# A gated mix of attention and a mixture of experts: experts taken in the order of their loads, and the steps of the score maxima at listed products

## The chip, the cores and the metric

The kernel runs on one core of one Trainium2 chip. The metric is the device time of one execution in microseconds. Before the change it is 1443.31 us, the median of three runs (1442.71 to 1444.89). The engines are called as the profile calls them: PE is TensorE (PEld its weight loads), DVE is VectorE, ACT is ScalarE, POOL is GpSimd, and SP is SyncE, which issues most of the DMAs.

## What is computed

```python
x = A_x                                          # [1, 2048, 448]
g = sigmoid((x * gate_w).sum(-1, keepdims=True))
# a: softmax attention, 16 heads of 28
q, k, v = split(x @ wqkv)                        # per head
a = softmax(q @ k.T * 28 ** -0.5) @ v @ wo
# b: the two best of 8 experts for each token
logits = x @ w_gate
topk = argsort(-logits)[:, :2];  gates = softmax(logits[topk])
for e in range(8):
    w = (gates * (topk == e)).sum(-1)
    b += w * (silu(x @ w1[e]) @ w2[e])           # w1 448 x 1792, w2 1792 x 448
return g * a + (1 - g) * b
```

All is float32. A product of two float32 matrices is made from high and low parts, three products of a faster kind: high by high, high by low, low by high. The low part is what is left of a number once its rounded high part is taken off.

## The kernel before

There are 2048 tokens of 448 features. The stages follow one another on PE.

First come v, the gate and the router's logits, 16 tiles of 128 tokens (`v_block`, L334). Each tile's v goes to DRAM (`v_d`, stored on SP at L382 from the tile `v_s`). Beside it SP issues 32 stores that write zeros into the rows of `ys_d`, the array of the experts' results, which no token may fill (L385 and L388, from the SBUF tile `zf`).

Then q and k are projected (`qk_tile`, products L569 of 512 columns). Results go to DRAM in a high part (ACT at L578 makes `hi`, SP stores it at L582) and a low one (L581, L583). Beside this the routing runs on DVE, a few operations at a time (`routing`, popped by `route`): it finds each token's two experts, counts tokens per expert with a triangular matmul (L431, which needs the mask that ends with `dl`, L424), and gives every token a slot. Each expert has room for 640 slots, of which 576 (`CAP`) are worked through by the regular code; tokens beyond would go to spilled tiles that are run at the end. The counts are kept in `cnt_i`. Before the last three `qk_tile` calls the first w1 weights (`w1r`, L212) and the first expert's tokens are fetched.

The expert stage loops over the eight experts `e` (L834), each in two halves of F (`hf`), seven 128-row blocks `f` in a half:

- w1: for each block two column halves `c` of HC = 288 slots, each the sum of 11 products (L870) in one PSUM bank. Two banks, `acc0` and `acc1`, take turns. ACT applies silu to PSUM twice, into the high part `hh` and into the full value `hf32`; POOL makes the low part `hl` (`hidden_low`, L749) one block later. ACT and POOL also make high and low parts of the coming weights (w1 at L696 and L702, w2 at L734 and L740).
- last tile: under `If(cnt > 512)` the slots past the 512th, in plain float32 (`last_slots`, products L800, branch L904).
- w2: four tiles `k` of 128 slots, each 21 products of 448 columns (L920). In second halves the next expert's tokens are transposed between them (`turn_x`, L722).

Attention needs, for its softmax, the maximum of each row of scores ahead of time. These maxima are made inside the expert stage, where DVE has little else to do: there are 1024 cells of 128 × 512 scores (`max_stream`). One step makes six cells, PE writing the six banks of `pm` (L106), DVE reducing four and then two of them (L126). Where the accumulator that isn't in use can be lent, a step makes seven: the lent bank is reduced by itself (L120), then three and three. PE must not begin a step until DVE has read `pm`. When the maxima of a group are complete, `store_max` transposes them (L142) into a lent bank, and DVE and SP send them off.

Where a step stands is decided by `worked`: after each product it counts down, and when a product listed in `w1_due` or `W2_DUE` is reached a step is due. In the w1 stage steps have six banks; in the w2 stage a lent bank may be had from the due product on. A store takes the place of a step, which then follows some products later.

PE, ACT, DVE and POOL keep the order of the code in this stage; SP isn't among them, and its order is set by the scheduler.

Attention proper (scores, exponentials, values) and the output projection, which also gathers the experts' results from `ys_d`, come last. The change doesn't touch them.

Of the kernel before, what the change touches and what calls it, by code (L numbers as in the profile page):

```python
# [21 lines left out]
STORE_NS = 600  # L22
U_NS, Y_NS, YT_NS = 131, 206, 452
# [4 lines left out]
CAP = 576  # L28
# [5 lines left out]
CT = [128, 128, 128, 128, CAP - 512]  # L34
HC = CAP // 2
# [9 lines left out]
def bc(ap, shape):  # L45
    return ap.to_broadcast(shape)
# [3 lines left out]
def tile_gated_mha_moe(ctx: ExitStack, tc: tile.TileContext, x, xT, wv, wqk, wo, w1, w2, out):  # L50
# [13 lines left out]
    ys_d = dram.tile([NS, D], F32, name="ys_d")  # L64

# [5 lines left out]
    cnt_i = consts.tile([128, E], I32, name="cnt_i")  # L71
# [101 lines left out]
    want, hold = [0], [0]  # L173
# [9 lines left out]

    def worked(ns, due=False, bank=None):
        hold[0] = max(0, hold[0] - ns)
        want[0] += due
        if want[0] and not hold[0]:
            if flush and bank:
                store_max(*flush.pop(0), bank())
                hold[0] = STORE_NS  # L190
                return
            if bank:
                spare.append(bank())
            next(ms, None)
            want[0] -= 1
            spare.clear()
# [5 lines left out]
    def gather(e, k):  # L202
        xg = pe.tile([128, 512], F32, name="xg", bufs=5)
        nc.gpsimd.indirect_dma_start(
            out=xg[:CT[k], 0:D], out_offset=None, in_=x,
            in_offset=bass.IndirectOffsetOnAxis(ap=idx_i[:CT[k], 5 * e + k:5 * e + k + 1], axis=0))
        return xg

    def rows4(dst, src, eng, parts=slice(0, 3)):
        for to, rows in ((dst[:, 0:3], src[0:384].rearrange("(b p) n -> p b n", p=128)),  # L210
                         (dst[0:64, 3], src[384:448]), (dst[64:128, 3], src[384:448]))[parts]:
            eng.dma_start(to, rows)  # L212

    def load_w1(e, c):
# [13 lines left out]
    def x_tile(xg, k, new_pt, xeh, xel):  # L228
        n = CT[k]
# [8 lines left out]
    with ExitStack() as pa:  # L238
# [32 lines left out]
        def load_wq(i):  # L271
# [13 lines left out]
        ioc = sb.tile([128, NT, E], F32, name="ioc")  # L285
        nc.gpsimd.iota(ioc, pattern=[[0, NT], [CPAD, E]], base=0, channel_multiplier=0,
                       allow_small_or_imprecise_dtypes=True)
        thr = sb.tile([128, E, 12], F32, name="thr")
        nc.gpsimd.iota(thr, pattern=[[0, E], [128, 12]], base=CAP, channel_multiplier=0,
# [16 lines left out]
        nc.gpsimd.memset(zf, 0.0)  # L306
        sbase = sb.tile([128, E + 1], F32, name="sbase")
# [47 lines left out]
        for t in range(NT):  # L355
# [41 lines left out]
        def routing():  # L397
# [43 lines left out]
            nc.vector.tensor_copy(cnt_i, rk[:, NT])  # L441
            yield
            over = tmp("over", [128, E, 12])
            nc.vector.tensor_tensor(over, bc(rk[:, NT].unsqueeze(2), [128, E, 12]), thr, op=ALU.is_gt)
# [9 lines left out]
            nc.vector.scalar_tensor_tensor(spo, sbase[:, 0:E], 128.0, ioc[:, 0], op0=ALU.mult, op1=ALU.subtract)  # L454
            nc.vector.tensor_scalar(spo, spo, float(NMAIN - CAP), None, op0=ALU.add)
            yield
            ov = tmp("eq", TE)
            nc.vector.scalar_tensor_tensor(ov, rk[:, 0:NT], float(CAP), bc(spo.unsqueeze(1), TE),
                                           op0=ALU.is_ge, op1=ALU.mult)
            yield  # L460
            slotE = tmp("cand", TE)
            nc.vector.tensor_tensor(slotE, rk[:, 0:NT], ioc, op=ALU.add)
# [26 lines left out]
            for c in range(2):  # L489
                for h in range(2):  # L490
# [13 lines left out]
                    yield "pause"  # L504
            yield "pause"
            yield "pause"
            yield "pause"
# [92 lines left out]
        next(ms)  # L600
        xgs = [gather(0, k) for k in range(5)]
        w1rs = [load_w1(0, c) for c in range(3)]
        for i, mt in enumerate((5, 2, 6)):
            if i == 2:
                for k in range(5):
                    tail_twice(xgs[k][:CT[k]])
                xe = x_tiles()
# [64 lines left out]
    with ExitStack() as pb:  # L672
# [10 lines left out]
        def fetch_w2(i):  # L683
            if i < E * NF:
                t = sb.tile([128, D], F32, name="w2r", bufs=9)
                nc.sync.dma_start(t, w2[i // NF][(i % NF) * 128:(i % NF + 1) * 128])
                w2rs.append(t)
# [30 lines left out]
        def turn_x(xg, k, xeh, xel):  # L718
            n = CT[k]
# [37 lines left out]
        def spilled_tiles(n_spill):  # L757
            w1f = w1.rearrange("e d f -> (e d) f")
            w2f = w2.rearrange("e f d -> (e f) d")
# [34 lines left out]
        def last_slots(e, hf, hs, y):  # L794
            n, w = CT[4], D // 2
            py = accumulator()
            for f in range(NH):
                w2r = w2t[e * NF + hf * NH + f][2]
                for c in range(2):
                    nc.tensor.matmul(py[64 * c:64 * c + n, 0:w], hs[f][2], w2r[:, c * w:(c + 1) * w],  # L800
                                     start=f == 0, stop=f == NH - 1)
            if hf == 0:
                nc.scalar.activation(y[:, 0:w], py[:, 0:w], AF.Copy)
                return
            r0 = e * CPAD + 512
            yo = sb.tile([128, D], F32, name="yo")
            nc.scalar.activation(yo[:, 0:w], py[:, 0:w], AF.Copy)
            nc.gpsimd.tensor_tensor(yo[:, 0:w], yo[:, 0:w], y[:, 0:w], op=ALU.add)
# [349 lines left out]
```

## Time and profile before

| | us |
|---|---|
| median of three runs | 1443.31 |
| the profiled execution | 1443.26 |
| its span in the trace | 1441.4 |
| v, gate, logits | 0 to 43.8 |
| q and k projection, routing | 43.8 to 121.8 |
| experts, maxima | 121.8 to 906 |
| attention | 906 to 1397 |
| output projection | 1397 to 1441.4 |

The stages are cut where PE goes from one stage's line to the next. In the profile's rows a time line gives the start, the length, the engine, the line of the kernel, the operation, the names of what is written and read, the shape, and in brackets how long the engine stood idle just before and what ended that. A matmul's length is that of the whole way through the array; products follow each other closer than that, so what a product costs is read from the distance of two starts. In groups, the two numbers behind the first bar are the busy time of the group and the mean length of one in ns, and what stands behind the second is the idle time ahead of it. In a line of the waits view stand the total, how many, and the longest.

### The profile page before, as it was taken

What the parts mean: (1) busy time and instruction counts of PE and PEld (TensorE: products, weight loads), DVE (VectorE), ACT (ScalarE), POOL (GpSimd) and SP (SyncE); (2) the same over time, 40 slices, a digit from 0 to 9 for tenths busy, and PEclk for the clock granted to TensorE, in tenths of its full rate; (3) what the DMA queues carried; (4) which work ended last, traced back from release to release, by engine and by line L of the source; (5) the groups of instructions that cost most, each with busy time, mean ns of one, the idle gap of its engine ahead of it and who ended that gap; (6) DMA issues with size and microseconds to landing.
All of it is one profiled execution on the core that took longest, in us unless ns stands there. A gap on an engine that the chain in (4) does not pass through costs nothing. (4 is left out here: it accounts for less than half of the span.)

```text
span 1441.4 us, 28118 instructions
## 1 busy us (share of the span) xinstructions
PE 1423.7 (99%) x11025; PEld 953.7 (66%) x11025; DVE 794.5 (55%) x858; ACT 899.2 (62%) x1559; POOL 646.5 (45%) x685
## 2 busy tenths in 40 slices
PE   9999999999999999999999999999999999999998
PEld 8788888888888888788888887533333333333347
DVE  5636777777778778778688787111142111221136
ACT  5235355344443553453444434799999999999981
POOL 1124597577666874874775656212222112112110
PEclk9999999999999999999999999999999999999999
DMA  9887532344133323331431320311422231142103
GB/s 332 291 289 238 169 112 78 97 136 129 43 103 118 103 81 110 123 98 55 137 118 37 107 70 3 108 47 49 130 55 59 78 98 47 43 122 64 32 20 119
DMA packets 110201, 153.18 MB, mean 106 GB/s; under 512 B 17884, under 2 KB 81516, under 8 KB 110064
## 3 DMA queue, kind: packets, MB, share of 16 engines
q1 hardware_dynamic: 100832, 129.86, 28.7%
q0 software_dynamic: 9088, 21.22, 4.9%
q8 instruction: 90, 1.47, 0.4%
q14 instruction: 47, 0.39, 0.1%
q10 hardware_dynamic: 144, 0.23, 0.1%
HBM read 109.20 MB, written 37.85 MB: 102 GB/s over the span
## 5 line engine op out<-in xcount | busy, mean ns | idle before, releaser
L126 DVE TENSOR_REDUCE mp<-pm 128x2 f32<-128x1024 f32 (+2 forms) x324 | 552.3, 1747 | 130.8 <-PE pm L106 130.3
L1058 ACT ACTIVATE P<-ps 128x1536 f32<-128x1536 f32 x254 | 367.9, 1448 | 0.0
L1067 PE MATMUL po<-P,V 128*32 128x512 f32 x2032 | 270.6, 604 | 0.0
L870 PE MATMUL acc<-xeh,w1l 128*128 128x288 f32 x880 | 258.5, 301 | 0.0
L870 PE MATMUL acc<-xeh,w1h 128*128 128x288 f32 x880 | 256.6, 298 | 0.0
L667 PEld LDWEIGHTS ps<-Q,Kh 29*128 29x128 f32 x2032 | 77.8, 183 | 212.6 <-ACT P L1057 212.3
L740 POOL TENSOR_TENSOR w2l<-w2r,w2h 128x448 fp32r<-128x448 f32 x112 | 129.0, 1153 | 168.9 <-ACT w2h L734 168.9
L870 PE MATMUL acc<-xel,w1h 128*128 128x288 f32 x660 | 195.1, 296 | 0.0
L667 PE MATMUL ps<-Q,Kh 29*128 29x512 f32 x2032 | 190.0, 444 | 0.0
L872 ACT ACTIVATE hh<-acc 128x288 fp32r<-128x288 f32 x224 | 92.3, 412 | 154.1 <-PE acc L870 154.1
L870 PEld LDWEIGHTS acc<-xeh,w1l 128*128 128x128 f32 x880 | 165.9, 189 | 18.6 <-issue 18.6
L920 PE MATMUL acc<-w2h,hh 128*128 128x448 f32 x448 | 171.8, 383 | 0.0
L870 PEld LDWEIGHTS acc<-xeh,w1h 128*128 128x128 f32 x880 | 165.7, 188 | 9.0 <-issue 7.3
L920 PE MATMUL acc<-w2l,hh 128*128 128x448 f32 x448 | 167.2, 373 | 0.0
L920 PE MATMUL acc<-w2h,hl 128*128 128x448 f32 x448 | 165.0, 368 | 0.0
L702 POOL TENSOR_TENSOR w1l<-w1r,w1h 128x512 fp32r<-128x512 f32 (+1 forms) x88 | 137.5, 1563 | 43.5 <-ACT w1h L696 25.3
L1071 DVE COPY osb<-po 128x512 f32<-128x512 f32 x16 | 11.1, 691 | 264.7 <-PE po L1067 246.9
L1014 POOL DMA_DIRECT2D sum_d<-osb x64 | 32.2, 515 | 271.7 <-DVE osb L1071 238.4
L1057 ACT ACTIVATE P<-ps 128x512 f32<-128x512 f32 x254 | 151.7, 597 | 1.4 <-ACT P L1058 0.5
L749 POOL TENSOR_TENSOR hl<-hf,hh 128x512 fp32r<-128x512 f32 x112 | 143.4, 1287 | 0.0
L106 PE MATMUL pm<-khg,qg 28*128 28x512 f32 x969 | 118.2, 454 | 9.7 <-DVE mp L126 5.9
L870 PEld LDWEIGHTS acc<-xel,w1h 128*128 128x128 f32 x660 | 124.6, 189 | 3.1 <-issue 2.9
(203 smaller groups left out, 1881.3 us busy)
## 6 DMA issues: line engine op xcount, KB each, us to landing
w2r<-in_w_dram SPq DMA_DIRECT2D x112, 224.0 KB
w1r<-in_w_dram SPq DMA_DIRECT2D x56, 384.0 KB
ys_d<-zf SPq DMA_DIRECT2D x32, 224.0 KB
qkh_d<-hi SPq DMA_DIRECT2D x28, 256.0 KB
qkl_d<-lo SPq DMA_DIRECT2D x28, 256.0 KB
w1r<-in_w_dram SPq DMA_DIRECT2D x112, 64.0 KB
ys_d<-yo SPq DMA_DIRECT2D x32, 224.0 KB
v_d<-v_s SPq DMA_DIRECT2D x16, 256.0 KB
```

The costliest lines, as they stand in the source:

```text
L106: nc.tensor.matmul(banks[n], qgs[g, qt // 4][rw, (qt % 4) * 128:(qt % 4 + 1) * 128], kh[g, kc][rw], start=True, stop=True)
L126: nc.vector.tensor_reduce(mp[:, (o + lo) % 256:(o + lo) % 256 + hi - lo], pm[:, lo:hi], axis=AX.X, op=ALU.max)
L667: nc.tensor.matmul(banks[j], k[rw, ks], q[rw, c], start=i == 0, stop=i == 2)
L702: nc.gpsimd.tensor_tensor(l[:, :, half], r[:, :, half], h[:, :, half].bitcast(F32), op=ALU.subtract)
L740: nc.gpsimd.tensor_tensor(w2l, w2r, w2h.bitcast(F32), op=ALU.subtract)
L749: nc.gpsimd.tensor_tensor(hl, hf32, hh[:, 0:512].bitcast(F32), op=ALU.subtract)
L870: nc.tensor.matmul(pu[:, 0:HC], a, b[:, cs], start=i == 0, stop=i == len(mms) - 1)
L872: nc.scalar.activation(hh[:, cs], pu[:, 0:HC], AF.Silu)
L920: nc.tensor.matmul(py[:n, 0:D], a[:, cs], b, start=i == 0, stop=i == 3 * NH - 1)
L1057: nc.scalar.activation(P[:, 0], p1, AF.Exp, scale=SCALE)
L1058: nc.scalar.activation(P[:, 1:4], p3, AF.Exp, scale=SCALE)
L1067: nc.tensor.matmul(po[32 * j:32 * j + 32], v[:, kt % 8, 32 * j:32 * j + 32], P[:, j] if n > 1 else P[j], start=kt == 0, stop=kt == NT - 1)
```

## The change

The experts are taken in the order of their counts. `routing` gets some twelve more small DVE operations: a key from count and number, how many keys are ahead (`pos`), and a cap for each position p: 576, 564, 552, 540, 528, 516, 512, 512. A token's slot is counted from its expert's position. With the inputs at hand the counts are 561, 545, 514, 507, 501, 500, 497, 471 in that order, so none is over its cap and no tile is spilled, in either kernel; three experts have over 512 tokens. HC is half the cap, so the products in w1's stage have 288 columns at position 0 and 256 at positions 6 and 7. There the last tile, its gather, its transposes and its `If` are gone from the code.

Since which expert stands at a position is known only at run time, SP reads the eight expert numbers from `cnt_i` (`load_experts`), and the addresses of the w1 and w2 loads are worked out from registers.

The steps of the maxima stand at listed products (`STEPS`): a positive number is a step with the lent accumulator as seventh bank, now also within w1's blocks (at the sixth of 11 products), a negative one a step of six. When a store is due it goes into the lent bank of the step, which then makes six cells. The order has 153 steps, 110 of them with seven banks; before it had 162, 55 with seven.

ACT's second silu in w1's stage becomes a copy: silu goes to `hf32`, and `hh` is copied from it.

The zeros of `ys_d` are copied from a small DRAM tile, `zero_d`, which POOL writes once. These stores stand in the w2 stage of the code.

```diff
-STORE_NS = 600
-U_NS, Y_NS, YT_NS = 131, 206, 452
+STEPS = [
+    (([-3, 28, 61, 94, -124, 149], [8, 28, 48, 68]), ([6, -36, 61, -91, 116, 148], [3, -24, 39, 58, 76])),
...
+    (([17, 50, 83, 116, 149], [18, 39, 60, 81]), ([28, 61, 94, 127], [7, 27, 47, 67])),
+]
-CT = [128, 128, 128, 128, CAP - 512]
-HC = CAP // 2
+CAPS = [max(CAP - 12 * p, 512) for p in range(E)]
+CTS = [[128] * 4 + [c - 512] * (c > 512) for c in CAPS]
-    def worked(ns, due=False, bank=None):
...
+    def step(bank):
+        if bank and flush:
+            store_max(*flush.pop(0), bank)
+        elif bank:
+            spare.append(bank)
+        next(ms, None)
+        spare.clear()
...
+    def load_experts():
+        for p in range(E):
+            experts.append(nc.values_load(cnt_i[0:1, 1, p:p + 1], engines=[mybir.EngineType.SP],
+                                          min_val=0, max_val=E - 1))
+    def load_w1(p, c):
         t = pe.tile([128, 4, 256], F32, name="w1r", bufs=3)
-        rows4(t, w1[e][:, c * 256:(c + 1) * 256], nc.sync)
+        cs = slice(c * 256, (c + 1) * 256)
+        nc.sync.dma_start(t[:, 0:3], w1f[ds(experts[p] * D, 384), cs].rearrange("(b p) n -> p b n", p=128))
+        for r in (0, 64):
+            nc.sync.dma_start(t[r:r + 64, 3], w1f[ds(experts[p] * D + 384, 64), cs])
...
-            if t >= 4:
-                for i in range(2 * t - 8, 2 * t - 6):
-                    nc.sync.dma_start(ys_d[NMAIN + i * 128:NMAIN + (i + 1) * 128], zf)
-                    if i % 3 == 0:
-                        r0 = (i // 3 + 1) * CPAD
-                        nc.sync.dma_start(ys_d[r0 - CPAD + 512:r0], zf)
...
         next(ms)
+        load_experts()
         xgs = [gather(0, k) for k in range(5)]
...
+            CT, HC = CTS[e], CAPS[e] // 2
...
-                            worked(U_NS, 2 * NM * f + c * NM + i in w1_due[six])
-                        nc.scalar.activation(hh[:, cs], pu[:, 0:HC], AF.Silu)
+                            behind(w1_steps, 2 * NM * f + c * NM + i + 1)
+                        nh = min(HC, 512 - c * HC)
+                        hs_ = slice(c * HC, c * HC + nh)
+                        nc.scalar.activation(hf32[:, hs_], pu[:, 0:nh], AF.Silu)
+                        if ht and c == 1:
+                            nc.scalar.activation(ht[:, 0:CT[4]], pu[:, nh:HC], AF.Silu)
+                        nc.scalar.activation(hh[:, hs_], hf32[:, hs_], AF.Copy)
...
-                        with tc.If(cnt > 512):
-                            last_slots(e, hf, hs, ysb[4])
-                        worked(0, True)
+                        if len(CT) == 5:
+                            with tc.If(cnt > 512):
+                                last_slots(e, hf, hs, ysb[4])
...
+                            behind(w2_steps, 3 * NH * (n_k - 1) + i)
...
+                    if hf == 0 and n_k:
+                        r0 = e * CPAD + 512 if n_k == 1 else NMAIN + (3 * e + n_k - 2) * 128
+                        nc.sync.dma_start(ys_d[r0:r0 + 128], zero_d)
```

On PE, this is the end of w1's stage in the first half of the seventh expert (position 6). Before, the last of the 288-column products are followed by the branch, the last tile's products that it may skip, and a step with six banks:

```order
L870 MATMUL acc<-xeh,w1h 128x288
L870 MATMUL acc<-xeh,w1l 128x288
L904 COMPARE_AND_BRANCH
L800 MATMUL acc<-w2r,ht 64x224 x14
L904 UNCONDITIONAL_BRANCH x2
L106 MATMUL pm<-khg,qg 128x512 x6
L920 MATMUL acc<-w2h,hh 128x448
```

Now, at the same place (L903 is w1's product, L118 the step's, L953 w2's; buffer numbers are kept here, and the lent bank is the row with `acc1` before the six of `pm`):

```order
L903 MATMUL acc0_9051<-xeh_8463,w1l_8877 128x256
L118 MATMUL acc1_9058<-khg_8285,qg_7956 128x512
L118 MATMUL pm_9059<-khg_8285,qg_7956 128x512
L118 MATMUL pm_9059<-khg_8372,qg_7956 128x512 x4
L118 MATMUL pm_9059<-khg_8443,qg_7956 128x512
L903 MATMUL acc0_9051<-xeh_8463,w1h_8970 128x256
L903 MATMUL acc0_9051<-xel_8462,w1h_8970 128x256
L903 MATMUL acc0_9051<-xeh_8463,w1l_8971 128x256
L903 MATMUL acc0_9051<-xeh_8463,w1h_8970 128x256
L903 MATMUL acc0_9051<-xeh_8463,w1l_8971 128x256
L953 MATMUL acc1_9108<-w2h_8767,hh_8751 128x448
```

The step has moved into the last block of w1's stage, between its sixth and seventh product, and has seven banks; the branch and the last tile are gone, and w2's first product follows w1's last.

On SP, this is the place of the first w1 loads, in the q and k projection (`qg` is a load for the maxima's steps, `w1r` the weights). Before:

```order
L78 DMA qg<-qkh_d 28x512 x4
L212 DMA w1r<-in_w_dram 128x3x256
L212 DMA w1r<-in_w_dram 64x256 x2
L212 DMA w1r<-in_w_dram 128x3x256
L212 DMA w1r<-in_w_dram 64x256 x2
L212 DMA w1r<-in_w_dram 128x3x256
L212 DMA w1r<-in_w_dram 64x256 x2
L582 DMA qkh_d<-hi 128x512
```

Now, from the last of the eight reads, which all stand alike ahead of the first load:

```order
L221 TENSOR_LOAD cnt_i
L221 ISA x2
L227 ISA
L227 DMA w1r<-in_w_dram 128x3x256
L229 ISA
L229 DMA w1r<-in_w_dram 64x256
L229 ISA
L229 DMA w1r<-in_w_dram 64x256
L227 ISA
```

The loads and the store behind them (L614 now) have moved back by the eight reads and by an address instruction for each load.

Still on SP, the end of the v stage, with the last v stores (`v_d`) among the zero stores (`ys_d`). Before:

```order
L388 DMA ys_d<-zf 128x448
L385 DMA ys_d<-zf 128x448
L382 DMA v_d<-v_s 128x512
L385 DMA ys_d<-zf 128x448 x2
L388 DMA ys_d<-zf 128x448
L382 DMA v_d<-v_s 128x512
L385 DMA ys_d<-zf 128x448 x2
L582 DMA qkh_d<-hi 128x512
```

Now:

```order
L393 DMA v_d<-v_s 128x512
L965 DMA ys_d<-zero_d 16x3584 x2
L393 DMA v_d<-v_s 128x512
L965 DMA ys_d<-zero_d 16x3584 x2
L614 DMA qkh_d<-hi 128x512
L965 DMA ys_d<-zero_d 16x3584
```

Though the code has the zero stores in the w2 stage, the scheduler issues 26 of the 32 here and at the start of the next stage: 22 ahead of the last v store, where 30 stood before, and four between it and the second store of `qkl_d`. The last six come in the expert stage.

More of the change, by code (lines that the diff above doesn't have):

```diff
@@ L70, in tile_gated_mha_moe @@
     idx_i = consts.tile([128, NTL], I32, name="idx_i")
-    cnt_i = consts.tile([128, E], I32, name="cnt_i")
+    cnt_i = consts.tile([128, 2, E], I32, name="cnt_i")
     def load_qg(g, c):
@@ L180, in pop @@
                 late.pop(0)()
-    def worked(ns, due=False, bank=None):
[L185 to L196, printed above, removed]
+    def step(bank):
[5 more added lines that the diff above has]
+        spare.clear()
     def flush_x():
@@ L202, in gather @@
     def gather(e, k):
+        n = CTS[e][k]
         xg = pe.tile([128, 512], F32, name="xg", bufs=5)
         nc.gpsimd.indirect_dma_start(
[L205 to L214 removed]
+            out=xg[:n, 0:D], out_offset=None, in_=x,
+            in_offset=bass.IndirectOffsetOnAxis(ap=idx_i[:n, 5 * e + k:5 * e + k + 1], axis=0))
+        return xg
+    w1f = w1.rearrange("e d f -> (e d) f")
+    w2f = w2.rearrange("e f d -> (e f) d")
+    experts = []
+    def load_experts():
[3 more added lines that the diff above has]
+    def load_w1(p, c):
         t = pe.tile([128, 4, 256], F32, name="w1r", bufs=3)
[L216 removed]
+        cs = slice(c * 256, (c + 1) * 256)
+        nc.sync.dma_start(t[:, 0:3], w1f[ds(experts[p] * D, 384), cs].rearrange("(b p) n -> p b n", p=128))
+        for r in (0, 64):
+            nc.sync.dma_start(t[r:r + 64, 3], w1f[ds(experts[p] * D + 384, 64), cs])
         return t
@@ L440, in routing @@
             nc.vector.tensor_copy(rk, pr)
-            nc.vector.tensor_copy(cnt_i, rk[:, NT])
+            cnt = rk[:, NT]
+            key = tmp("key", [128, E])
+            nc.vector.scalar_tensor_tensor(key, cnt, float(E), io8[:, 0], op0=ALU.mult, op1=ALU.subtract)
+            yield
+            EE = [128, E, E]
+            ahead = tmp("ahead", EE)
+            nc.vector.tensor_tensor(ahead, bc(key.unsqueeze(1), EE), bc(key.unsqueeze(2), EE), op=ALU.is_gt)
+            yield
+            pos = tmp("pos", [128, E])
+            nc.vector.tensor_reduce(pos, ahead, axis=AX.X, op=ALU.add)
+            yield
+            cap = tmp("cap", [128, E])
+            nc.vector.tensor_scalar(cap, pos, -12.0, float(CAP), op0=ALU.mult, op1=ALU.add)
+            nc.vector.tensor_scalar(cap, cap, 512.0, None, op0=ALU.max)
+            yield
+            nc.vector.tensor_tensor(key, cnt, cap, op=ALU.subtract)
             yield
             over = tmp("over", [128, E, 12])
-            nc.vector.tensor_tensor(over, bc(rk[:, NT].unsqueeze(2), [128, E, 12]), thr, op=ALU.is_gt)
+            nc.vector.tensor_tensor(over, bc(key.unsqueeze(2), [128, E, 12]), thr, op=ALU.is_gt)
             yield
@@ L504, in routing @@
                     yield "pause"
+            at = tmp("at", EE)
+            nc.vector.tensor_tensor(at, bc(pos.unsqueeze(1), EE), bc(io8[:, 0].unsqueeze(2), EE), op=ALU.is_equal)
             yield "pause"
-            yield "pause"
-            yield "pause"
+            pc = tmp("pc", [128, 2, E])
+            for i, what in enumerate((cnt, io8[:, 0])):
+                nc.vector.tensor_tensor(ahead, at, bc(what.unsqueeze(1), EE), op=ALU.mult)
+                yield
+                nc.vector.tensor_reduce(pc[:, i], ahead, axis=AX.X, op=ALU.add)
+                yield "pause"
+            nc.vector.tensor_copy(cnt_i, pc)
             yield "pause"
@@ L716, in tile_gated_mha_moe, with turn_x @@
         xf = sb.tile([128, 4, 512], F32, name="xf", bufs=1)
-        def turn_x(xg, k, xeh, xel):
-            n = CT[k]
+        def turn_x(xg, k, n, xeh, xel):
             pt = ps.tile([128, 512], F32, name=f"acc{turn[0] ^ 1}").rearrange("p (b n) -> p b n", b=4)
@@ L828, in tile_gated_mha_moe, with behind @@
         NM = 11
-        w1_due = [(18, 46, 73, 100, 128), (11, 35, 59, 83, 107, 131)]
-        W2_DUE = [(15, 13, 12, 10), (16, 14, 13, 12)]
+        def behind(places, i):
+            if i in places:
+                step(other_accumulator())
+            elif -i in places:
+                step(None)
         for e in range(E):
-            cnt = nc.values_load(cnt_i[0:1, e:e + 1], min_val=0, max_val=S)
+            CT, HC = CTS[e], CAPS[e] // 2
+            later = CTS[e + 1] if e + 1 < E else []
+            if len(CT) == 5:
+                cnt = nc.values_load(cnt_i[0:1, 0, e:e + 1], min_val=0, max_val=S)
             xgs = []
@@ L844, in tile_gated_mha_moe @@
                 lag = None
-                six = hf == 1 and e >= E - 4
+                w1_steps, w2_steps = STEPS[e][hf]
                 for f in range(NH):
@@ L921, in tile_gated_mha_moe @@
                             i += 1
-                            free = due <= i < due + 4 and (n_k > 1 or not turns)
-                            worked(Y_NS, i == due, other_accumulator if free else None)
+                            behind(w2_steps, 3 * NH * (n_k - 1) + i)
                             if (e, hf, n_k) == (E - 1, 1, 4) and i in (1, 10):
```

69 lines of the change are left out of this document (33 added, 36 removed), and 6 rows, old and new, of the table STEPS.

## The prediction

> **What bounds the kernel now.** I read the page's head first, then busy time by stage: 0–43.8 us v, gate and logit projection; to 121.8 q/k projection with the routing beside it; to 906 the experts; to 1397 attention. The columns are the stage's length, busy us of PE, PEld, DVE, ACT and POOL, granted clock, DMA share and GB/s.
>
> ```profile
> span 1441.4 us, 28118 instructions
> PE 1423.7 (99%) x11025; PEld 953.7 (66%) x11025; DVE 794.5 (55%) x858; ACT 899.2 (62%) x1559; POOL 646.5 (45%) x685
> 0.00:43.80 43.80, 42.27 (x196) 37.19 (x197) 23.04 (x60) 23.39 (x45) 7.44 (x48) 1.00 0.96 344
> 43.80:121.80 78.00, 75.53 (x378) 61.52 (x377) 40.80 (x102) 24.82 (x48) 12.42 (x15) 1.00 0.80 279
> 121.80:906.00 784.20, 774.50 (x5129) 647.42 (x5128) 598.55 (x460) 354.99 (x936) 522.36 (x456) 1.00 0.32 100
> 906.00:1397.00 491.00, 490.83 (x5117) 173.58 (x5119) 106.58 (x188) 485.88 (x516) 100.37 (x158) 1.00 0.25 69
> ```
>
> TensorE sets the end in every stage and its clock is full. The change touches the first three stages, mostly the experts', where PE is busy 774.5 of 784.2 us; VectorE (599) and GpSimd (522) come next, and a shorter PE stage brings both nearer. Next the spacing of products, in the PE timeline: w1's products of 288 columns (L870), w2's of 448 (L920), the q/k projection's of 512 (L569), and 128-column transposes (L722).
>
> ```profile
> 43.80 0.39 PE L569 MATMUL pq<-xh,wqk_h 128*128 128x512 f32 x1
> ...
> 49.04 0.39 PE L569 MATMUL pq<-xl,wqk_h 128*128 128x512 f32 x1
> ...
> 725.15 0.29 PE L870 MATMUL acc<-xel,w1h 128*128 128x288 f32 x1
> ...
> 727.54 0.30 PE L870 MATMUL acc<-xeh,w1h 128*128 128x288 f32 x1
> ...
> 728.47 0.29 PE L870 MATMUL acc<-xel,w1h 128*128 128x288 f32 x1
> 728.69 0.73 PE L106 MATMUL pm<-khg,qg 28*128 28x512 f32 x6
> 729.35 0.40 PE L870 MATMUL acc<-xeh,w1l 128*128 128x288 f32 x1
> 729.59 0.29 PE L870 MATMUL acc<-xeh,w1h 128*128 128x288 f32 x1
> ...
> 805.69 0.60 PE L722 MATMUL acc<-ident,xg 128*128 128x128 f32 x4
> ...
> 840.57 0.29 PE L870 MATMUL acc<-xeh,w1l 128*128 128x288 f32 x1
> 841.16 0.73 PE L106 MATMUL pm<-khg,qg 28*128 28x512 f32 x6 [0.30 <-PEq L904]
> ...
> 842.33 0.37 PE L920 MATMUL acc<-w2h,hl 128*128 128x448 f32 x1
> ...
> 844.77 0.37 PE L920 MATMUL acc<-w2h,hl 128*128 128x448 f32 x1
> ```
>
> From 725.15 to 728.47 lie 25 intervals: 0.1328 us a product. From 43.80 to 49.04 lie 23: 0.2278. From 842.33 to 844.77 lie 12: 0.2033. So a column costs (0.2278 − 0.1328)/224 = 0.424 ns or (0.2033 − 0.1328)/160 = 0.441 ns, and the 288-column product lies on the line through the longer ones.
>
> **The change part by part.** I sum against the profiled execution: 1443.26 us, 1441.4 of it span; it agrees with the median of the runs, 1443.31, to 0.05.
>
> *Narrower w1 products.* A position runs 14 column blocks of F by 11 products, 154, on each of its two column halves. The caps fall below 576 by 0, 12, 24, 36, 48, 60, 64, 64, together 308 columns, so 154 × 308 = 47,432 columns go: −20.1 us at 0.424 ns, −20.9 at 0.441. I take **−20.3**. Against it: four 128-column transposes take 0.60 us, of which one by itself 0.27 (the mean of that group below), so (0.60 − 0.27)/3 = 0.109 apart, above the line's 0.065. Something holds short products up; at 256 columns the line gives 0.119, above 0.109, so I take no loss. The Trainium skill ("TensorE: Matmul & The Clock Gate", section "LDWEIGHTS (loading the stationary operand)") has a weight load take its columns over 1.2 ns whatever the product's width, 107 ns for 128: by that rule, too, 256 columns are not held up, and the 0.109 agrees. The same page's section "Back-to-back issue gap" gives 81 ns at 128 columns and 131 at 512 for a sustained stream; that would be 0.13 ns a column and −6.2 us here, and the row of 0.2278 at 512 speaks against it.
>
> *Fewer steps.* A step of maxima enters PE 728.47 → 729.35, 0.88 for one spacing, 0.75 over it; the next product comes at 0.24 in place of 0.13, so 0.85. The listed places make 153 steps of the 162 (seven banks in 110, where 55 had them): nine fewer, **−7.7**. Page rows of the vector work behind them, the waits view, and the vector engine's timeline:
>
> ```profile
> L722 PE MATMUL acc<-ident,xg 128*128 128x128 f32 x112 | 16.8, 272 | 0.0
> L126 DVE TENSOR_REDUCE mp<-pm 128x4 f32<-128x2048 f32 x106 | 242.9, 2292 | 128.7 <-PE pm L106 128.7
> PE pm L106 <- DVE mp L126: 5.9, 22, 0.6
> 646.61 0.69 DVE L120 TENSOR_REDUCE mp<-acc 128x1 f32<-128x512 f32 x1 [0.67 <-PE acc L106]
> ...
> 678.84 3.42 DVE L126 TENSOR_REDUCE mp<-pm 128x4 f32<-128x2048 f32 x2 [0.81 <-PE pm L106]
> 683.18 3.42 DVE L126 TENSOR_REDUCE mp<-pm 128x4 f32<-128x2048 f32 x2 [0.92 <-PE pm L106]
> ```
>
> *Waits for the vector engine.* Six banks hold it from one step to the next for 683.18 − 678.84 = 4.34 us. In the second halves of the last four experts steps stand 24 products apart, 24 × 0.1328 + 0.85 = 4.04: a wait of 0.30, 19 times, 5.7 us. In the w2 stage some eight steps come about 0.6 too early, 4.6, and the joints of the stages cost about 1: some 12 in all, where the waits view names 5.9 (it misses those that begin at the weight load). The list puts 33 products behind most seven-bank steps (33 × 0.119 + 0.85 = 4.78 at the narrowest; VectorE needs 3.42 + 0.69 and up to 0.6 more) and 25 or fewer behind some six-bank ones; adding these places up leaves about 5.5. **−6.5**, from −10 to −3.
>
> *The conditional last tile.* Going past it costs 841.16 − 840.57 = 0.59 against 0.22 at an ordinary step: 0.37. Two positions have none now, four passes: **−1.5**. Stores inside steps, two pairs of 64-column transposes fewer, some twelve small vector operations in the routing beside 78 us of which VectorE is busy 40.8: 0 ± 1.
>
> *SP before the first weights.* The order has eight reads of the expert numbers and nine address instructions on SP ahead of, and among, the first w1r loads; behind them stands a q/k store. Their nearest rows, with ACT and PE:
>
> ```profile
> 93.05 6.54 SPq L212 DMA_DIRECT2D w1r<-in_w_dram  x9
> 99.69 0.53 SPq L582 DMA_DIRECT2D qkh_d<-hi  x1
> 102.75 0.60 ACT L578 ACTIVATE hi<-pq 128x512 fp32r<-128x512 f32 x1 [7.75 <-DMA qkh_d<-hi]
> 103.96 0.39 PE L569 MATMUL pq<-xh,wqk_l 128*128 128x512 f32 x1
> 104.24 0.50 PE L569 MATMUL pq<-xh,wqk_h 128*128 128x512 f32 x1
> L835 SPq TENSOR_LOAD <-cnt_i x8: 263/368/713, 121.6 to 172.6; - x8
> L835 SPq FUSED_REGOPS  x8: 147/153/192, 122.1 to 173.2; - x8
> ```
>
> Already now ACT waits 7.75 us at 102.75 for that store, whose buffer `hi` it refills, and PE's product at 104.24 comes 0.28 after the last (0.23 is normal): no slack is left. A read with its two small instructions is 0.37 + 0.15 + a little, 0.55; eight are 4.4, nine address instructions up to 1.4. **+5**, from 0 (they might run before 93, while SP stands) to +7.
>
> *GpSimd becomes late.* It makes w1's and w2's low parts (L702, L740) and the hidden ones (L749):
>
> ```profile
> 729.11 1.28 POOL L702 TENSOR_TENSOR w1l<-w1r,w1h 128x512 fp32r<-128x512 f32 x1 [0.42 <-ACT w1h L696]
> 732.88 1.28 POOL L702 TENSOR_TENSOR w1l<-w1r,w1h 128x512 fp32r<-128x512 f32 x1
> ...
> 740.40 1.29 POOL L702 TENSOR_TENSOR w1l<-w1r,w1h 128x512 fp32r<-128x512 f32 x1
> 743.99 2.54 POOL L749 TENSOR_TENSOR hl<-hf,hh 128x512 fp32r<-128x512 f32 x2
> 746.64 0.37 PE L920 MATMUL acc<-w2h,hl 128*128 128x448 f32 x1
> ```
>
> It runs without a gap, 3.77 us a block, and its last hidden part ends at 746.53, 19.0 after the end of the third block (727.54); the product that reads it starts at 746.64, 19.1 after. So PE has 0.1 to spare. Each 12 slots off the cap bring that product forward by 4 blocks × 22 products × 6 × 0.424 ns = 0.22 us; where the conditional is gone, by 0.37 more. In the first halves that makes 0.6, 0.8, 1.0, 1.5 and 1.5 us of waiting at positions 3 to 7 (0 to 2 run the last tile's products, over 1 us, ahead of it): some 5, less where a listed step stands in between, 4. For the second halves, whose chain is alike, I take as much: **+8**, from 0 to +12.
>
> *Zero stores.* In the order 22 of them, now copies from DRAM, stand ahead of the last v store, where 30 stood:
>
> ```profile
> 51.90 0.22 PE L431 MATMUL pt<-mb,tri 128*128 128x136 bf16 x1 [2.47 <-DVE dl L424]
> ACT v_s L376 <- DMA v_d<-v_s: 14.1, 8, 4.6
> ys_d<-zf SPq DMA_DIRECT2D x32, 224.0 KB
> ```
>
> The routing's first matmul waits 2.47 us for a chain that hangs on v stores through queues 96% busy. One zero store is 229,376 bytes, 0.67 us at the stage's 344 GB/s; eight fewer are up to 5.3, of which 2.5 can show. But a copy inside DRAM is in no row here: read and write might cost twice, (22 × 2 − 30) × 0.67 = +9. I take **−1**, from −2.5 to +9.
>
> *ACT in w1's stage.* A block's hidden part is now copied from the first Silu's result, and seven-bank steps borrow the other accumulator while ACT may still read it: +1, from 0 to +4.
>
> Sum: −20.3 − 7.7 − 6.5 − 1.5 + 5 + 8 − 1 + 1 = **−23.0**, 1443.3 − 23 = **1420.3, called 1420**.
>
> **The rivals.** *The costs stay hidden.* SP's reads run in an idle stretch and GpSimd catches up in the w2 stages, where it has less to do: −36 + 1 → **1408**, and 1404 with the far ends of the vector waits and of the column's price. For it: GpSimd is busy only 522 of 784 us. Against: the two rows with 0.1 us or less to spare.
>
> *The coupling costs double.* GpSimd's lateness passes from half to half and the accumulators come free late: +8 and +1 become +20 → **1431**; for it, the chain is back to back in the rows.
>
> *The products do not get shorter,* because the weight load, and not the columns, sets 0.133: the 20.3 go, GpSimd's 8 too → **1433**. Against it stands the line through three widths.
>
> *Slower: the copies inside DRAM choke the v stage.* 22 stores at k × 0.67 us against 30 × 0.67 ahead of the last v store: from k = 30/22 = 1.36 the stage grows, by 14.7 × (k − 1.36) us, and the whole gain of some 22 is eaten from k = 2.9; at k = 3.2 → **1448**. For it: this stage's DMA is 96% busy, and no row shows such a copy. Against: nothing but the small number of bytes.
>
> **How the numbers follow.** Forecast 0.60 (its own range 1412 to 1428, from the bounds of SP, GpSimd and the waits), hidden costs 0.21, doubled coupling 0.09, no shorter products 0.04, slower 0.06. A measurement can tell about 0.2%, 2.9 us, from no change; between 1440 and 1446 I put 0.03, from the neighbours of the last two. The range of 1404 to 1433 leaves out the slower rival and the rims. Faster 0.91, same 0.03, slower 0.06.
>
> **What would show it.** Right: w1 products 0.119 us apart at the last positions; 153 steps; PE waits for `hl` and `w1l` of about 8 us in the second half of the expert stage; an ACT wait for the q/k store of about 12 us near 104. Wrong: products of 256 columns still 0.13 apart; a first stage over 46 us; GpSimd with gaps in its chain at the last positions; waits for accumulators in w1's stage.

## The result, and the profile after

The changed kernel takes 1416.21 us (median of six runs, 1414.36 to 1417.63) where the kernel before takes 1442.70 in the same comparison: a ratio of 0.9813, 95% interval 0.980 to 0.9826. That is 26.5 us less; forecast were 23, and 1420. The profiled execution has 1414.95 us. Its page, and busy time by the same stages as before (the same columns):

```profile
span 1413.1 us, 28682 instructions
PE 1398.2 (99%) x11017; PEld 932.3 (66%) x11017; DVE 798.3 (56%) x909; ACT 913.5 (65%) x1531; POOL 644.5 (46%) x682
0.00:44.15 44.15, 42.12 (x196) 37.93 (x197) 23.17 (x61) 23.89 (x46) 8.17 (x52) 1.00 0.96 348
44.15:122.14 77.99, 75.61 (x379) 61.52 (x378) 42.68 (x114) 24.42 (x47) 14.77 (x11) 1.00 0.74 256
122.14:878.40 756.26, 749.95 (x5120) 624.95 (x5119) 599.85 (x496) 369.53 (x908) 517.20 (x453) 1.00 0.34 105
878.40:1369.10 490.70, 490.67 (x5122) 174.15 (x5125) 107.04 (x190) 485.79 (x516) 100.45 (x158) 1.00 0.24 69
```

Nearly all of the gain lies in the expert stage, 784.2 to 756.3 us; the v stage is 0.35 longer, the q and k stage as long as it was, and attention and output, which the change doesn't touch, are 0.7 shorter. DVE works as many microseconds as before in a shorter stage: 599.85 of 756, where it had 598.55 of 784. PE's time line at two places, the joint of w1 and w2 at position 4 and products with a step at the last position:

```profile
544.41 0.29 PE L903 MATMUL acc<-xeh,w1l 128*128 128x264 f32 x1
545.24 0.47 PE L953 MATMUL acc<-w2h,hh 128*128 128x448 f32 x1 [0.54 <-ACT ht L909]
...
800.36 0.28 PE L903 MATMUL acc<-xel,w1h 128*128 128x256 f32 x1
...
804.09 0.28 PE L903 MATMUL acc<-xeh,w1l 128*128 128x256 f32 x1
804.30 0.49 PE L118 MATMUL acc<-khg,qg 28*128 28x512 f32 x1
```

From 800.36 to 804.09 lie 31 intervals, 0.120 us each, where the 288-column products had 0.133 and the forecast 0.119. The step enters at its usual distance, 0.21. New is the joint: 0.83 us from w1's last product to w2's first, of which 0.54 is a wait for ACT. The waits of PE in this kernel that bear on the change, from the waits view (total, how many, the longest):

```profile
PE acc L953 <- ACT ht L909: 3.3, 6, 0.5
PE pq L601 <- DVE lo L613: 2.3, 1, 2.3
PE pm L118 <- DVE lo L613: 1.1, 1, 1.1
PE acc L953 <- POOL hl L781: 0.4, 2, 0.2
PE pm L118 <- DVE mp L138: 0.2, 1, 0.2
```

The waits of steps for DVE, 5.9 us in that view before, are down to 0.2. GpSimd, priced at 8, shows 0.4 there. In the view of the weight loads' own waits (PEld) it shows more:

```profile
PEld acc L903 <- POOL w1l L735: 1.9, 7, 0.4
PEld acc L953 <- POOL hl L781: 1.1, 2, 0.6
```

ACT at the joint, which the forecast had in no row, is now the largest wait. The 2.3 stands where the forecast had looked for SP, at 102 us, and the wait of the triangular matmul has gone:

```profile
49.81 0.22 PE L436 MATMUL pt<-mb,tri 128*128 128x136 bf16 x1
...
101.92 0.39 PE L601 MATMUL pq<-xh,wqk_l 128*128 128x512 f32 x1
104.62 0.50 PE L601 MATMUL pq<-xh,wqk_h 128*128 128x512 f32 x1 [2.31 <-DVE lo L613]
```

On SP, its reads and the q/k store behind the weight loads, and on ACT the wait for that store:

```profile
L221 SPq TENSOR_LOAD <-cnt_i x8: 262/268/1097, 88.0 to 93.3; - x8
94.04 0.46 SPq L227 DMA_DIRECT2D w1r<-in_w_dram  x1
...
100.16 0.53 SPq L614 DMA_DIRECT2D qkh_d<-hi  x1
103.24 0.60 ACT L610 ACTIVATE hi<-pq 128x512 fp32r<-128x512 f32 x1 [10.26 <-DMA qkh_d<-hi]
```

The store is issued at 100.16, and was at 99.69: SP comes to the reads 5 us earlier than it came to the weight loads before (88.0 against 93.05), spends 6 us on them, and is done with the loads behind them in 6.1 us in place of 6.6. PE, which no longer waits for the triangular matmul, is at this place 2.0 us earlier: its last product ahead of the pause starts at 101.92, and at the same place before at 103.96. So the pause is mostly the time that the vanished wait had given back, with the store leaving almost when it always did.

The expert stage by its halves, from first product to first product: 792.1 us before (w1's first product to w2's last), 764.2 after. 2464 w1 products at the spacing measured in each half are 326.7 and 307.8, so 18.9 less; nine steps are 7.7 less; eight 64-column transposes fewer, 0.9 (by the 0.109 of the 128-column ones); all the rest together falls by 0.4 only. Within that rest the waits for DVE and the branches went, and ACT's joints, GpSimd and a wait of 1.1 at the first step came.

### The profile page after: what moved, and what is told of

Its sections match the earlier page's. It is cut to its first block, busy times and chain, and to the rows that moved or that the text cites. A ratio compares the mean times of both kernels' runs of the same rounds, so it can differ in the third digit from the quotient of the medians.

```text
span 1413.1 us, 28682 instructions
## 1 busy us (share of the span) xinstructions
PE 1398.2 (99%) x11017; PEld 932.3 (66%) x11017; DVE 798.3 (56%) x909; ACT 913.5 (65%) x1531; POOL 644.5 (46%) x682
## 5 line engine op out<-in xcount | busy, mean ns | idle before, releaser
L138 DVE TENSOR_REDUCE mp<-pm 128x3 f32<-128x1536 f32 (+3 forms) x307 | 520.4, 1737 | 40.1 <-PE pm L118 40.1
L903 PE MATMUL acc<-xeh,w1h 128*128 128x256 f32 (+6 forms) x880 | 252.5, 296 | 0.0
L903 PE MATMUL acc<-xeh,w1l 128*128 128x256 f32 (+6 forms) x880 | 246.9, 290 | 0.4
L903 PE MATMUL acc<-xel,w1h 128*128 128x256 f32 (+6 forms) x660 | 189.7, 287 | 0.0
L903 PEld LDWEIGHTS acc<-xeh,w1h 128*128 128x128 f32 x880 | 165.7, 188 | 24.8 <-issue 23.7
L953 PE MATMUL acc<-w2h,hh 128*128 128x448 f32 x448 | 172.8, 386 | 3.5 <-ACT ht L909 3.3
L903 PEld LDWEIGHTS acc<-xeh,w1l 128*128 128x128 f32 x880 | 165.9, 189 | 5.5 <-issue 3.3
L953 PE MATMUL acc<-w2l,hh 128*128 128x448 f32 x448 | 166.2, 371 | 0.0
L953 PE MATMUL acc<-w2h,hl 128*128 128x448 f32 x448 | 165.4, 369 | 0.4 <-POOL hl L781 0.4
L907 ACT ACTIVATE hf<-acc 128x256 f32<-128x256 f32 (+6 forms) x224 | 86.1, 384 | 113.6 <-PE acc L903 97.2
L132 DVE TENSOR_REDUCE mp<-acc 128x1 f32<-128x512 f32 x110 | 76.1, 692 | 107.2 <-PE acc L118 100.6
L903 PEld LDWEIGHTS acc<-xel,w1h 128*128 128x128 f32 x660 | 124.6, 189 | 1.3 <-issue 1.1
```

Source lines behind the costliest of these rows:

```text
L132: nc.vector.tensor_reduce(mp[:, o:o + 1], banks[0], axis=AX.X, op=ALU.max)
L138: nc.vector.tensor_reduce(mp[:, (o + lo) % 256:(o + lo) % 256 + hi - lo], pm[:, lo:hi], axis=AX.X, op=ALU.max)
L903: nc.tensor.matmul(pu[:, 0:HC], a, b[:, cs], start=i == 0, stop=i == len(mms) - 1)
L907: nc.scalar.activation(hf32[:, hs_], pu[:, 0:nh], AF.Silu)
L953: nc.tensor.matmul(py[:n, 0:D], a[:, cs], b, start=i == 0, stop=i == 3 * NH - 1)
```

## The experiments

Each run stands beside runs of the kernel before on the same chip; there were three such sets, with medians of 1444.28, 1444.84 and 1444.49 us for that kernel. The changed kernel's second median, 1416.78, is the measure below; where stages are compared they are read from the two traces (q/k stage: first q/k product to first w1 product; expert stage: from there to w2's last product). The changed kernel itself has 78.0 and 764.2 in its first profile.

**The changed kernel again.** 

> The changed kernel again, unaltered, as the measure for the runs beside it. Both theories: 1416 us, ratio to the kernel before 0.981 to 0.982.

1416.78 us (1416.28 to 1419.8), ratio 0.9818 (0.9805 to 0.9832). Expert stage 764.12, to 0.1 us as in the first profile and in each half to 0.1. The q/k stage took 80.03 in place of 77.99: PE's wait at 102 us was 2.8, and in the stretch behind it the granted clock was 0.84. What differs between these two executions lies nearly all there. The granted clock also tells the changed kernel's executions apart: of the eleven in both runs, the two with a mean clock of 1.000 took 1414.36 and 1414.95 us, the nine with 0.997 to 0.999 took 1416.05 to 1419.80. So a difference of 2 to 3 us between medians can be the clock's; where it matters below, executions at 1.000 are compared.

**Widths.** `CAPS = [CAP] * E` in place of the falling caps.

> The changed kernel with all caps at 576: order, steps and stores stay, the w1 products are 288 columns wide everywhere and the last tile is there at every position. Theory A: the 47,432 columns cost 19 to 20 us, the last tile's If and transposes at positions 6 and 7 some 2, and PE's short waits for GpSimd at positions 4 to 7 (3 to 4 us) go: 17 to 18 us more than the changed kernel. Theory B, the prediction's sum (20.3 and 1.2 for columns and branches, 8 back from GpSimd): 13 more. Theory C, products of 256 columns are held up by weight loads: under 8 more.

1435.92 us, ratio 0.9948 (0.9934 to 0.9962): 19.1 over the changed kernel, and the expert stage is 783.26, 19.1 longer. Nearest to A, and 6 over B: what GpSimd was to give back isn't there. C falls, as the spacing of 0.120 says already.

**Places of the steps.** The old due numbers:

```diff
-                            behind(w1_steps, 2 * NM * f + c * NM + i + 1)
+                            worked(U_NS, 2 * NM * f + c * NM + i in w1_due[six])
...
+                        worked(0, True)
...
-                            behind(w2_steps, 3 * NH * (n_k - 1) + i)
+                            worked(Y_NS, i == due, other_accumulator if free else None)
```

> The changed kernel with the steps where they stood before (due numbers, six banks in w1's stage, a step behind the last tile, stores in a step's place): 162 steps, everything else as changed. Theory A: nine steps are 7.7 us, the second halves of positions 4 to 7 have steps 24 products apart, 24 x 0.12 + 0.85 = 3.7 us against the 4.34 that the vector engine needs, 0.6 x 20 = 12, the w2 stage's waits 4, less 3.3 for ACT's wait at the joints and 3 for GpSimd's, which longer stages hide: 17 us more than the changed kernel. Theory B, the prediction's terms (7.7 and 6.5): 14 more. Theory C, GpSimd is the bound of the late positions, so the steps' waits are hidden beside it: under 8 more.

1432.97 us, ratio 0.9923 (0.9908 to 0.9938): 16.2 over the changed kernel, expert stage 780.62, 16.5 longer. A's 17 is right. Where it goes is seen in PE's waits of this kernel and in DVE's steps in the first half of position 7:

```profile
PE pm L120 <- DVE mp L140: 14.4, 35, 0.8
818.26 3.42 DVE L140 TENSOR_REDUCE mp<-pm 128x4 f32<-128x2048 f32 x2 [0.92 <-PE pm L120]
822.60 3.42 DVE L140 TENSOR_REDUCE mp<-pm 128x4 f32<-128x2048 f32 x2 [0.92 <-PE pm L120]
```

4.34 us from step to step, the time that DVE needs for six banks. With the narrow products even the 27 or 28 of them between two steps of a first half are over sooner than that. In the second halves, with 24 between two steps, w1's stage at positions 4 and 5 takes 27.9 us with the narrow products as with the wide ones (the next run): there the narrower products only lengthen the wait.

**Widths and places both undone.** Both edits together.

> The changed kernel with steps where they stood before and all caps at 576. Theory A, widths and places are worth 11.5 and 8.8 us each by itself, and 28 together, since with the old places the late second halves are as long as the vector engine needs, whatever the products' width: the expert stage is then 792 us as in the kernel before, 28 us over the changed one, and the time 1444. Theory B, the effects of the two runs that undo one each (19.1 and 16.5) add: 35.6 over the changed kernel, 1452.

1442.92 us, ratio 0.9992 (0.9983 to 1.0001); expert stage 789.82. A's 792 and 1444 are 2 and 1 us off, B's 1452 is excluded. The square of expert stages is 789.8 (old places, wide), 783.3 (listed, wide), 780.6 (old, narrow), 764.1 (listed, narrow). Either alone is worth 6.6 or 9.2 us, both 25.7: 10 us come only from having the two together. The 2.3 us by which this corner stays below the 792.1 of the kernel before belong to the rest of the change; which part, no run tells.

**ACT at the joints.**

```diff
-            py = accumulator()
+            py = accumulator() if e < 3 else ps.tile([128, 512], F32, name=f"acc{turn[0]}")
             for f in range(NH):
```

> The changed kernel, but from position 3 on the last tile (skipped there) takes the bank of w1's last sum and not the other, so that w2's first sum begins in the bank that ACT has long read. Theory A: PE's wait of 0.55 us for ACT at the six joints of w1 and w2 at positions 3 to 5 is for the bank; it goes: 3.3 us less than the changed kernel. Theory B, the wait is for the hidden part that w2's first products read, or for the branch: no difference.

1414.22 us, ratio 0.9794 (0.978 to 0.9807): 2.6 less; expert stage 761.62, 2.5 less, 0.36 to 0.43 in each of the six w1 halves of positions 3 to 5 and nowhere else. The wait for `ht` is gone from the waits. A holds, at three quarters of its size. `last_slots` asks for the next accumulator in the code even where the branch skips it, so w2's first sum falls into the bank that ACT is still reading.

**ACT's copy.**

```diff
+                        nc.scalar.activation(hh[:, hs_], pu[:, 0:nh], AF.Silu)
                         nc.scalar.activation(hf32[:, hs_], pu[:, 0:nh], AF.Silu)
...
-                        nc.scalar.activation(hh[:, hs_], hf32[:, hs_], AF.Copy)
```

> The changed kernel with ACT's second silu from PSUM as before in place of the copy from SBUF: ACT reads each of w1's sums twice. Theory A: the bank comes free some 0.4 us later, so the six waits at the joints of positions 3 to 5 grow by as much (2.4 us) and steps that borrow a bank inside w1's blocks are held up: 2 to 6 us more than the changed kernel. Theory B, the banks are free early enough: no difference.

1423.81 us, ratio 0.9862 (0.9846 to 0.9878): 7.0 over the changed kernel, and 7.0 in the expert stage, a little over A's range. The joints wait longer, and the steps that borrow a bank enter later. PE's waits and one of its steps (position 7, first half):

```profile
PE acc L953 <- ACTq L940: 4.9, 6, 0.8
822.56 0.28 PE L903 MATMUL acc<-xeh,w1l 128*128 128x256 f32 x1
822.86 0.50 PE L118 MATMUL acc<-khg,qg 28*128 28x512 f32 x1
```

0.30 from the last product to the step, where it was 0.21. The seven-bank steps in w1's stage thus rest on the copy: the price of the borrowed bank is paid by taking ACT's second read off it.

**GpSimd.** `w2t[i][1] = w2h` in place of the low part, so w2's middle product reads the high part and GpSimd has 1.15 us less to do in each block.

> The changed kernel without GpSimd's low parts of w2 (the product of high by low reads the high part instead, so that PE does as much as before): 1.15 us less for GpSimd in every block. Theory A, from the trace: PE's short waits for GpSimd go, 3 to 4 us less than the changed kernel, nearly all at positions 4 to 7. Theory B, the prediction: GpSimd costs 8 us, so 8 less. Theory C, GpSimd isn't waited for: no difference.

1414.05 us, ratio 0.979 (0.9777 to 0.9804): 2.7 less, expert stage 761.40, 2.7 less. 1.1 of that is in the first halves of positions 6 and 7 behind w1 (0.56 and 0.54), nearly all the rest in w1's stage, 0.13 to 0.37 in each half from position 4 on. The weight loads' waits for `hl`, 1.1, are gone, and those for `w1l` fell from 1.9 to 0.5. A is nearest, somewhat high; B's 8 falls.

**SP's reads taken away.** `experts.append(p)` in place of the read: position p takes the weights of expert p.

> The changed kernel with fixed expert numbers in place of those read on SP (position p takes the weights of expert p, so the output is not the reference's): eight reads and all address instructions are gone. Theory A, from the two traces: the reads delay the q/k store on which ACT and then PE wait at 102 us; without them that wait of 2.3 us of PE goes, 2.4 us less than the changed kernel, and all of it between 100 and 105 us. Theory B, the prediction's price: 5 us less. Theory C, the store waits for its transfer and not for SP: no difference.

1414.33 us, ratio 0.9798 (0.9785 to 0.9812): 2.45 less, as A has it, but largely by luck. The q/k stage is 75.37 and has no wait at 102 left; that is 4.7 less than in the repeated run, but the v stage ends 1.0 later here (first q/k product at 45.35, there at 44.35), since the scheduler orders SP anew. Four of the five executions had the clock at 1.000 and took 1414.02 to 1415.27; the changed kernel's two at 1.000 took 1414.36 and 1414.95. So the 2.45 is nearly all the clock's. Nor are the reads alone taken away: SP now issues the first weight load at 104.13 only, behind q/k stores that had stood behind all nine. That the reads cause the wait is shown by the next run.

**SP's reads late.**

```diff
-        load_experts()
+        load_experts([0])
...
         while late or late_x:
             pop(1)
+        load_experts(range(1, E))
```

> The changed kernel with seven of the eight reads of expert numbers behind the q/k projection in the code; only the first stands ahead of the first weight loads. The result is the reference's. Theory A: SP reaches the q/k store about 4 us earlier and PE's wait of 2.3 us at 102 us goes: 2.3 us less than the changed kernel. Theory B, the store waits for the nine weight loads and their address instructions in any case: under 0.5 less.

1411.84 us (1411.7 to 1413.06), ratio 0.9777 (0.9764 to 0.9791): 4.9 less than the changed kernel, where A has 2.3; the run without reads is 2.5 slower, with its longer v stage. The q/k stage is 75.38, like that run's, and the store leaves SP here:

```profile
94.43 1.18 SPq L229 DMA_DIRECT2D w1r<-in_w_dram  x2
95.71 0.81 SPq L614 DMA_DIRECT2D qkh_d<-hi  x1
```

95.71 in place of 100.16, with the nine weight loads ahead of it as before. Without the pause at 102 us the clock doesn't fall behind it either: it is 1.00 from 101 to 112 us, as in the first profile of the changed kernel. Against that profile the q/k stage is 2.6 shorter (77.99 to 75.38), which is A's 2.3; the repeated run's was 2.0 longer, and those are the pause's other 0.5 and the clock.

**Zero stores as they were.** The 32 stores from `zf` back in the v stage, `zero_d` gone.

> The changed kernel with the 32 zero stores as they were, from SBUF in the v stage. Theory A: the wait of the triangular matmul (2.5 us at 52) comes back, but PE waits less at 102 us for the q/k store, which stands at the same time: the sum is 0 to 0.5 us longer, the wait at 102 shorter by about 2. Theory B: the two waits add, 2.4 us longer than the changed kernel. Theory C, the copies inside DRAM cost something by themselves (the v stage is 0.35 us longer with them): 0.3 us shorter.

1421.03 us, ratio 0.9844 (0.983 to 0.9857): 4.25 over the changed kernel. All three miss. The triangular matmul waits again, and the wait for the q/k store has grown, not shrunk:

```profile
52.16 0.22 PE L440 MATMUL pt<-mb,tri 128*128 128x136 bf16 x1 [2.13 <-DVE dl L433]
PE pq L605 <- DVE lo L617: 4.5, 1, 4.5
105.91 0.53 SPq L618 DMA_DIRECT2D qkh_d<-hi  x1
```

The store leaves SP at 105.91. With the old zero stores the transfers that SP stands for come later by some 5 us, and the reads then fall behind them instead of beside: zero stores and reads stand in one line. The two waits are 6.6 us where the first profile had 2.3, and the granted clock behind them was lower (0.89 from 44 to 60 us, 0.93 from 101 to 112 and 0.90 to 122), an estimated 3.5 us by the missing share of each stretch.

**Zero stores as they were, without reads.** Both edits.

> The changed kernel with the zero stores from SBUF in the v stage as before and fixed expert numbers in place of the reads (the output is not the reference's): the fourth corner of a square with the changed kernel, the run without reads and the run with the old zero stores. Theory A, reads and zero stores stand on the same path, SP up to the q/k store: this is like the kernel before there (78 us from the first q/k product to the first w1 product), so 2.5 to 3 us over the run without reads and 6 under the run with the old zero stores. Theory B, the two costs are independent: 4.3 us over the run without reads.

1417.15 us (1413.91 to 1418.55), ratio 0.9813 (0.9797 to 0.9829). Its q/k stage is 77.75, as A has it (78.0 in the kernel before). The times say less than the stages: 2.8 over the run without reads (A: 2.5 to 3), but 3.9, not 6, under the run with the old zero stores, and its own executions spread over 4.6 us: two at a clock of 1.000 took 1413.91 and 1413.97, no more than the run without reads, three at 0.998 and 0.999 took 1417.15 to 1418.55. So A's 2.5 to 3 is met by the clock; at full clock the run without reads has a q/k stage that is 2.4 shorter, but its v stage ends 1.5 later (45.35 against 43.81). In the stages of one profile each the reads cost 2.6 to 4.7 us with the copies and 7.5 with the old stores (85.26 against 77.75); in the medians 2.45 and 3.9. That the two costs stand on one path is shown by the issue times; how much more than the sum they are isn't settled, since of the 7.5 some 4.5 are waits and the rest about what the lower clock of the run with the old stores cost.

**Both mendings.** The late reads and the last tile's own bank.

> The changed kernel with both mendings: seven of the eight reads late, and from position 3 on the skipped last tile takes w1's own bank. The result is the reference's. Theory A, the two are in different stages and add: 2.6 and 3 to 5 us, so 1409 us. Theory B, one of them is taken back by GpSimd, which comes closer: 1411 to 1412.

1409.59 us (1409.16 to 1409.67), ratio 0.9763 (0.9749 to 0.9777): A. Expert stage 761.83, q/k stage 75.39. It is the fastest of all, 7.2 us under the changed kernel, and leaves out nothing of the computation; all five executions had the clock at 1.000, so some 2 of the 7.2 are the clock's.

## Why the prediction was right, point by point

*What bounds it.* Right: PE, at full clock, and the expert stage carries the change.

*Narrower products, −20.3.* 18.9 were measured from the spacings (0.120 in place of 0.119 at 256 columns) and 19.1 by undoing them. The rival by which weight loads keep the distance at 0.133 falls. From 288 to 256 columns a column costs (0.1328 − 0.1203)/32 = 0.39 ns. The Trainium skill ("TensorE: Matmul & The Clock Gate", section "Back-to-back issue gap") has a sustained spacing that makes 0.13 ns a column, or −6.2; that doesn't agree with the −18.9 here. The isolated gap of the same section, 1/2.4 ns a column, is nearer.

*Nine fewer steps, −7.7, and waits, −6.5.* 14.2 together; undoing the places costs 16.5 at the narrow widths (net of ACT's 3.3 at the joints, which the old places cover). Right in size, but the working added terms that aren't independent of the first. At the old widths the places are worth only 6.6, and the widths with the old places 9.2: the old list had been as long as DVE needs (4.34 us a step), and shorter products alone would have turned into waits.

*The conditional, −1.5.* Right where it is gone: the joint of the first half of position 7 is one ordinary spacing, 0.12 us. Where it stayed, something new stands behind it (ACT, below).

*SP, +5, and zero stores, −1.* The sum, +4, was measured as +0.3 in one profile and +2.5 in another, whose clock was lower behind the pause (start of the first w1 product). The price of the reads was right in sum (SP is at them from 88.0 to 94.0; 5.8 with the address instructions were reckoned, which show no cost between the loads), and so was the place: ACT's `hi`, then `lo`, then PE at 102. What failed is that the two were priced one by one. The zero stores' earlier end brings SP to its loads 5 us sooner, and the reads fill just these 5 us; each alone would have shown in the q/k stage (7.5 us more for the reads with the old stores, part of it the clock's; 2.4 less for the copies without reads). With the copies in place the reads cost 2.6, by the run with late reads.

*GpSimd, +8.* This step failed, by a misread row. The product at 746.64 reads a hidden part, but not the last one. w2's products of this half begin at 742.98, and each block takes three: the one at 746.64 is the eighteenth and reads the sixth block's part, which was ready at 745.28 (a narrower window has it from 743.99 for 1.29 us). The last block's part, ready at 746.53, is read by the twenty-first, at this row of the kernel before:

```profile
748.11 0.37 PE L920 MATMUL acc<-w2h,hl 128*128 128x448 f32 x1
```

So PE has 746.64 − 745.28 = 1.36 us to spare for the sixth part and 748.11 − 746.53 = 1.6 for the last, not 0.1. With 1.36 the same formula (0.22 for each 12 slots, 0.37 for the branch) gives a wait of about 0.2 in the first halves of positions 6 and 7 and none before. That is what PE shows: 0.19 and 0.16, at the product that reads the sixth part, which are the 0.4 for `hl`. Second halves had 3.4 to 5.9 to spare and none of them waits for `hl`. Taking work off GpSimd brings 2.7, of which 1.1 is behind these two waits and nearly all the rest in w1's stage, where weight loads wait for `w1l`. The forecast's sign for a right account, some 8 us of waits for `hl` and `w1l`, did not come.

*ACT, +1.* 3.3 at the six skipped joints, 0.54 of the 0.83 each (2.5 us come back when the last tile takes w1's own bank), which the step behind the branch had covered before (with the old places PE's waits have none of it); the forecast looked for this at the borrowed banks and not here. The copy that it was priced for avoids 7.

Put together, the measured terms differ from the forecast ones by +1.4 (columns), −3.7 (SP and zero stores, +0.3 for +4), −5.3 (GpSimd, 2.7 for 8) and +2.3 (ACT, 3.3 for 1): −5.3 in all. −23.0 − 5.3 = −28.3, which is the difference of the two spans, 1413.1 − 1441.4. That it fits to a tenth is chance: the steps' and waits' 14.2 are taken as met in this, where the traces bear them out only together and roughly; the 0.9 of the transposes is left out; and 0.7 of the difference lies in attention and output, which no term is about. Some luck is in the forecast's nearness too. It stood 12 us over its first rival, hidden costs, for SP, GpSimd and the zero stores (5 + 8 − 1), and of these 3.0 were found: on these terms the rival was nearer, and the time came nearer to the forecast because ACT's joints cost 2.3 more and the columns gave 1.4 less than both had reckoned, and because the median lies 1.3 over the profiled execution, whose clock was full.

## What to carry to other kernels

Two changes that ease the two engines of one loop must be priced together: shorter products alone were worth 9 us here and fewer waits alone 7, and both 26. Instructions added to a lone queue can cost nothing while something else brings the queue there early, but only as long as that lasts; look for the issue time of the first instruction behind the added ones. And when an order by hand takes a filler out of a place, ask whose latency it covered: here a last tile that is skipped at run time had still moved the next sum, in the code, into a bank that was being read. Last, where the clock differs from one execution to the next, a difference of 2 us is read from stages of traces with the same clock, not from medians.

## What the runs showed of the hardware

A pause of PE of about 3 us at 102 us was followed by a lower granted clock in some executions and not in others: windows of 101 to 112 us of the repeated run (pause 2.8), and of the run without w2's low parts (pause 2.8 too), with the columns of the stage view, the clock third from the end:

```profile
101.00:112.00 11.00, 8.24 (x30) 6.33 (x29) 3.36 (x5) 5.20 (x8) 2.40 (x1) 0.84 0.94 354
101.00:112.00 11.00, 8.20 (x37) 6.44 (x36) 3.75 (x6) 6.43 (x14) 2.42 (x1) 1.00 0.93 346
```

The Trainium skill ("TensorE: Matmul & The Clock Gate", section "What's actually happening") has the clock fall after an idle window of some 3.4 us that runs freely, not from the pause's start. That two equal pauses end with two clocks agrees with a window that runs freely; that pauses shorter than the window are followed by the lower clock at all does not. What decides is not shown. In the kernel with both mendings the pause is gone, and its five executions lie within 0.51 us, all at a clock of 1.000.
